# A Fourier mixing layer and a squared-ReLU FFN in one kernel: four steps of the third block and two more of the fourth in the halved form, the first folds and the even tables' weights in earlier steps

## The chip, the cores and the metric

The kernel runs on one core of a Trainium2 chip. The core has five engines, each with its own queue of instructions: PE (TensorE, the matrix engine), ACT (ScalarE), DVE (VectorE), POOL (GpSimd) and SP (SyncE), which here only issues stores. PE writes its sums to PSUM; ACT and DVE take them from there to SBUF, the on-chip memory. The metric is the device time of one launch in microseconds (us); lower is better.

## What is computed

The input x holds 8 batches of 3008 rows of 256 values. Each batch goes through a Fourier transform along the rows and one along the columns, of which only the real part is kept; the result goes row by row through two matrices (256 to 2048 and back) with a squared ReLU between them.

```python
X = np.fft.fft(x, axis=1)
X = np.fft.fft(X, axis=2)
x = X.real.reshape(B * S, D)          # 24064 x 256
h = np.maximum(x @ w_in, 0.0)         # 24064 x 2048
out = h * h @ w_out                   # 24064 x 256
```

## The kernel before

**Symmetry.** The real part of the transform of row k and that of row S - k are made of the same two sums, a cosine part P and a sine part Q: P + Q for one and P - Q for the other, up to the reversal of a row. So the kernel computes only 12040 columns (zc for the cosine part, zs for the sine part, of half of the columns each), and every column gives two output rows, an upper one and a mirrored one. The second transform is folded into the first matrix: `gh[:, 0]` and `gh[:, 1]` multiply zc and zs, and `gh[:, 2]` is `gh[:, 1]` with the factor that turns P + Q into P - Q (`turn2`). One output column needs a weight for a row of its own, `wv`, made by `row_weights` (L615).

**Blocks.** The 12040 columns go through 25 windows, here called blocks: `FIRST` gives 240, 512, 376, 376, 512, 448 columns (w = 0 to 5), then 512 each. The loop over `w` (L736) holds the whole order of work. A block has eight steps; step s makes 256 of the 2048 hidden values for all columns of the block. Between its matmuls stand those of other work, emitted by `others(s)` (L855): the jobs in `at[s]`, a slice of the second FFN matrix for the block before (`f2`, L667, sums po), the jobs in `post[s]`, and from step `lo` to `hi` a slice of the z jobs (L524, sums pz), which make zc and zs of a unit that the next block needs. Each engine takes its instructions in the order in which they are emitted.

**The plain step** (`pq`, `square`, `turn`): four matmuls (L787, L788) make P + Q in the sums ph, ACT takes them out with a ReLU (L797), two matmuls more (L793, the "turn") make P - Q of them in place, and ACT takes these out too. The squares of both are made by DVE (L802), but for the steps in `by_act`, where ACT squares the first half (L800). So a plain step has six matmuls as wide as the block, two evictions and two squares.

**The halved step** (`half_q`, `half_p`, `row_sum`, `halves`): two matmuls make Q alone, ACT takes it out as -2Q (`sn`, L820), two more add P, and ACT takes out P + Q (`hd`, L828). DVE makes P - Q by adding sn to hd (L850), takes the ReLU of both halves (L851) and squares them (L852). Ahead of that it adds the row of its own: `row` (L836) multiplies `eb` by a weight from `wv`, once for each 128 hidden values, and one add (L840) puts the rows on sn. Halved steps are grouped, in pairs at most, and DVE's three large operations are done once for a group, in the step after its last one. `eb` is the first row of zs spread over all partitions by a transfer that POOL issues (`row_spread`, L629), one for each block that has halved steps.

**Which steps.** `PLAN` (L60) maps a number to (groups of halved steps, steps with an ACT square), and `plan(w)` (L719) picks the number: none for w < 3, `PLAN[3]` for w = 3, that is (1, 2) and (4) halved and 0, 5, 6 squared by ACT, and `PLAN[2]` for w = 4, (2, 3) halved. In blocks 0 and 4, and in block 1, steps go in twos (`ng = 2`, L888).

**Folds and tables.** Each batch is loaded by POOL's queue into `xo` and folded by DVE along both axes (`fold_steps`, L376). The even half goes through DRAM and back (`even`, `back`, tile `rb`), and four last folds (`late`: two `fold8` L447, two `fold16` L458, and POOL's four small copies `nyq8` L464 to L466 into xt and spn) make what the z jobs of the even units read. The first batch's last folds stand in steps 3 to 6 of the third block (w = 2), the second's in steps 0 to 3 of the fifth (w = 4). `table_steps` (L244) makes the tables of sine and cosine for the even units, also in the third block: frequencies and arguments in step 0, turns (1), mods (2), absm (3), sine and cosine on ACT (4, 5), and the weights `weigh` (L285) in step 7. `row_weights` (16 matmuls, L619, and one DVE operation) stands in step 2.

**The z jobs.** `z_steps` (L504) makes one unit: for each part (0 cosine, 1 sine) and each half h a chain of matmuls. After h = 0 ACT copies the sums out (`es`, L529), after h = 1 it takes them out as zc or zs (L533), and DVE makes the mirrored columns from both (`minus`, L540). The order of parts and halves is one list for all units (L779): (1, 0), (0, 0), (1, 1), (0, 1). Of the even units, the sine part reads `spn` and the cosine part doesn't.

Of the kernel before, what the change touches and what calls it, by code (L numbers as in the profile page):

```python
# [28 lines left out]
def kernel(  # L29
# [30 lines left out]
    PLAN = {  # L60
# [5 lines left out]
    }  # L66

    RQ = (1, 3, 5, 0, 2, 4)
# [20 lines left out]
    def win_of(col):  # L89
        return max(w for w in range(NW) if wins[w][0] <= col) if col < TOT else NW  # L90
# [483 lines left out]
    f0s = fold_steps(0)  # L574
# [127 lines left out]
    folds = {0: f0s}  # L702

    def fold_jobs(i):
        f = folds[i] = fold_steps(i)
        return [f["d_even"], f["n_cos"], f["d_odd"], f["n_sin"], f["odds"], f["nyq"], f["even"], f["back"]]
# [11 lines left out]

    def plan(w):  # L719

        if w < 3:
            return (), ()
        if w < 5:
            return PLAN[3 if w == 3 else 2]
        first, late, main = w in first_at, w in late_at, w in fold_at
        n = 4 if main or late else 5 if first or w + 1 == NW or not need[w + 1] else 6
        return PLAN[n - (first and late)]

    def halved(w):

        return plan(w)[0]
# [4 lines left out]
    for w in range(NW):  # L736
# [4 lines left out]
        lo, hi = 0, NST - 2 if w == 3 or w > 4 else NST - 1  # L741
        at = [[] for _ in range(NST)]
        post = [[] for _ in range(NST)]
        if w == 0:
            at[7] = [f0s["even"], f0s["back"]]
        elif w == 1:
            fj = fold_jobs(1)
            at = [fj[0:1], fj[1:3], fj[3:4], fj[4:5], [], [], [], []]
            post[5] = fj[5:6]
            lo, hi = 6, 7  # L750
        elif w == 2:
            te = table_steps()
            at = [[folds[1]["even"], lambda: te["freq"](), lambda: te["args"](0)], [lambda: te["turns"](0)], [lambda: te["mods"](0)],
                  [lambda: te["absm"](0)], [lambda: te["sins"](0)], [lambda: te["coss"](0)], [], [lambda: te["weigh"]()]]
            for st in range(4):
                at[st + 3] = at[st + 3] + f0s["late"][st : st + 1]
            at[7].append(folds[1]["back"])
        elif w in fold_at:
            fj = jobs_of.pop(fold_at[w])
            at = [fj[2:3], fj[3:4], fj[4:5], [], [], [], fj[6:7], fj[7:8]]  # L760
            post[6] = fj[5:6]
        elif w == win_of(col_of[1, 1]) - 1:
            for st in range(4):
                at[st] = folds[1]["late"][st : st + 1]
            lo = 4
# [4 lines left out]
        if w in first_at:  # L770
            fj = jobs_of[first_at[w]] = fold_jobs(first_at[w])
            at[0] = at[0] + fj[0:1]
            at[1] = at[1] + fj[1:2]
        if w == 2:
            at[2].append(row_weights)
        zj, zl = [], []
        for u in need[w + 1]:
            zu = z_steps(u)
            zj += [(zu, 1, 0), (zu, 0, 0), (zu, 1, 1), (zu, 0, 1)]  # L779
        f2 = ffn2_steps(*old) if old else []  # L780
        phs = {}

# [20 lines left out]

        two = {s: g for g in halved(w) for s in g}
        by_act = plan(w)[1]
        sns, hds = {}, {}

# [178 lines left out]
```

## Time and profile before

| | before |
|---|---|
| median of 3 runs | 599.42 us (599.3 to 599.54) |
| the profiled execution | 599.14 us |
| its span | 597.4 us |
| busy PE, DVE, ACT, POOL | 97%, 86%, 86%, 17% of the span |
| granted TensorE clock | 0.999 |
| third block (w = 2), first L787 to the next block's | 48.27 to 70.28 us |
| fourth block (w = 3) | 70.28 to 89.93 us |
| fifth block (w = 4) | 89.93 to 112.55 us |

The profile is that of one execution. It times every instruction of each engine and says for idle time what ended it, by the semaphores. Lines such as L852 are those of the kernel below the heading above; a tile's name stands without its buffer number. Matmuls are pipelined: one that is listed with 0.32 us starts 0.16 us after the one ahead of it, and their ends are modelled, so that PE's busy time says only where it had work. The chain of waits follows the last instruction back to what released it, step by step, and so names what set the time at each moment. The time of a run is some 1.7 us more than the span of its instructions.

### The profile page before, as it was taken

The page shows a single profiled execution, that of the slowest core. Times are in us where ns is not written, and L with a number is a line of the kernel's source. Part 1 is how long each engine was busy: PE and PEld are TensorE (multiplying, and loading weights), DVE is VectorE, ACT ScalarE, POOL GpSimd, SP SyncE. Part 2 cuts the span into 40 slices and gives each one's busy share as a digit, 9 for nine tenths or more (in the row PEclk, how much of TensorE's full clock was granted, in tenths as well). Part 3 has the DMA queues.
Part 4 walks back from the last instruction along what each step waited for, and adds up shares of the span by engine and source line. Part 5 has one row for each costly group of instructions (what it writes and reads, how often), then busy time and mean ns, then how long its engine had stood idle before and what let it go on. Part 6 is the DMA issues. An engine that isn't in the chain of part 4 may idle for free.

```text
span 597.4 us, 11345 instructions
## 1 busy us (share of the span) xinstructions
PE 578.5 (97%) x4376; PEld 420.0 (70%) x4376; DVE 512.4 (86%) x748; ACT 514.3 (86%) x662; POOL 98.6 (17%) x152
## 2 busy tenths in 40 slices
PE   5899999999999999999999999999999999999996
PEld 2567776776777677777677777777777776776786
DVE  7897578886999987989889899898998799889980
ACT  7786888889999889989989898989989888888882
POOL 6350301202102023030112200403000120000000
PEclk9999999999999999999999999999999999999999
DMA  8955431562444536734455424555133351434122
GB/s 149 203 116 132 78 45 53 69 143 88 64 49 94 134 89 87 118 111 60 44 129 110 88 41 59 110 115 97 45 34 69 74 95 41 54 54 43 62 58 68
DMA packets 37581, 50.31 MB, mean 84 GB/s; under 512 B 4567, under 2 KB 30711, under 8 KB 37527
## 3 DMA queue, kind: packets, MB, share of 16 engines
q0 software_dynamic: 10400, 24.94, 32.1%
q1 hardware_dynamic: 26899, 24.44, 13.5%
q8 instruction: 34, 0.56, 0.4%
q10 hardware_dynamic: 228, 0.21, 0.1%
q14 instruction: 20, 0.16, 0.1%
HBM read 33.63 MB, written 27.84 MB: 103 GB/s over the span
## 4 chain that ended last, share of the span: by engine, by line
PE 66%; DVE 14%; ACT 11%; issue 7%; DMA 1%; POOL 0%; ACTq 0%; DVEq 0%; SPq 0%; POOLq 0%
PE po L667 39%; PE ph L826 5%; PE ph L812 5%; PE ph L793 4%; PE ph L787 4%; PE ph L788 4%; ACT h L797 3%; PE pz L524 3%; ACT sn L820 3%; DVE h L852 2%; ACT osb L682 2%; DVE hd L851 2%; ACT hd L828 2%; DVE hd L850 2%; DVE h L802 1%
## 5 line engine op out<-in xcount | busy, mean ns | idle before, releaser
L667 PE MATMUL po<-wout,h 128*128 128x256 f16 (+1 forms) x3024 | 362.0, 273 | 1.1 <-DVE h L852 1.1
L667 PEld LDWEIGHTS <-h 128*128 128x128 f16 (+1 forms) x3024 | 296.3, 98 | 73.0 <-DVE h L852 1.7
L797 ACT ACTIVATE h<-ph 128x1024 f16<-128x1024 f32 (+3 forms) x196 | 185.6, 981 | 11.6 <-PE ph L793 8.6
L828 ACT ACTIVATE hd<-ph 128x1024 f16<-128x1024 f32 (+3 forms) x94 | 94.0, 1001 | 14.7 <-PE ph L826 13.3
L852 DVE TENSOR_TENSOR h<-hd 128x4096 f16<-128x4096 f16 (+6 forms) x51 | 105.4, 2066 | 1.4
L802 DVE TENSOR_TENSOR h<-h 128x1024 f16<-128x1024 f16 (+3 forms) x135 | 85.4, 657 | 23.9 <-ACT h L797 22.4
L820 ACT ACTIVATE sn<-ph 128x1024 f16<-128x1024 f32 (+3 forms) x94 | 93.6, 997 | 0.7 <-PE ph L812 0.7
L840 DVE TENSOR_TENSOR sn<-sn,hd 128x2048 f16<-128x2048 f16 (+6 forms) x51 | 56.7, 1113 | 22.7 <-ACT sn L820 19.8
L682 ACT ACTIVATE osb<-po 128x512 f32<-128x512 f32 (+3 forms) x95 | 54.6, 578 | 24.6 <-PE po L667 23.9
L787 PE MATMUL ph<-zc,gh 128*128 128x512 f16 (+3 forms) x196 | 72.1, 368 | 0.5 <-ACT h L883 0.3
L788 PE MATMUL ph<-zs,gh 128*128 128x512 f16 (+3 forms) x196 | 72.1, 369 | 0.0
L850 DVE TENSOR_TENSOR hd<-hd,sn 128x2048 f16<-128x2048 f16 (+6 forms) x51 | 56.7, 1111 | 14.0 <-ACT hd L828 13.0
L800 ACT ACTIVATE h<-h 128x1024 f16<-128x1024 f16 (+3 forms) x61 | 62.7, 1028 | 1.9
L851 DVE TENSOR_SCALAR hd<-hd 128x4096 f16<-128x4096 f16 (+6 forms) x51 | 56.8, 1113 | 1.5
L826 PE MATMUL ph<-zc,gh 128*128 128x512 f16 (+3 forms) x188 | 54.6, 372 | 3.4 <-ACT sn L820 2.5
L793 PE MATMUL ph<-zs,gh 128*128 128x512 f16 (+3 forms) x196 | 55.3, 368 | 0.2 <-ACT h L797 0.2
L812 PE MATMUL ph<-zs,gh 128*128 128x512 f16 (+3 forms) x188 | 54.5, 373 | 0.0
L836 DVE TENSOR_SCALAR hd<-eb,wv 128x512 f16<-128x512 f16 (+3 forms) x188 | 54.0, 347 | 0.3 <-DMA eb<-zs 0.3
L788 PEld LDWEIGHTS <-gh 128*128 128x128 f16 x196 | 19.1, 97 | 21.2 <-issue 1.0
L787 PEld LDWEIGHTS <-gh 128*128 128x128 f16 x196 | 19.1, 97 | 20.3
L812 PEld LDWEIGHTS <-gh 128*128 128x128 f16 x188 | 18.3, 97 | 20.9
L629 POOL DMA_DIRECT2D eb<-zs x22 | 13.3, 603 | 117.4 <-ACT zs L533 59.4
(145 smaller groups left out, 418.0 us busy)
## 6 DMA issues: line engine op xcount, KB each, us to landing
out_dram<-osb SPq DMA_DIRECT2D x77, 128.0 KB
xo<-in_x_dram POOLq DMA_DIRECT2D x7, 768.0 KB, 7.3
scr<-ev POOLq DMA_DIRECT2D x8, 390.0 KB, 4.8
eb<-zs POOLq DMA_DIRECT2D x19, 128.0 KB, 7.0
rb<-scr POOLq DMA_DIRECT2D x16, 130.0 KB, 2.6
out_dram<-osb SPq DMA_DIRECT2D x12, 94.0 KB
w<-in_moe_w_in_dram POOLq DMA_DIRECT2D x2, 512.0 KB, 9.8
wout<-in_moe_w_out_dram POOLq DMA_DIRECT2D x1, 1024.0 KB, 11.8
```

Of the source, the lines that this page charges most:

```text
L667: nc.tensor.matmul(po[0:m, j * D : (j + 1) * D], h2[:, fc, q : q + m], wout16[:, fc, :], start=(fc == 0 and (j == 0 or not four or i > 3)) ...
L787: nc.tensor.matmul(ph[:, a, 0:wn], gh[:, 0, f0 : f0 + P], zcw[:, 0:wn], start=True, stop=False)
L788: nc.tensor.matmul(ph[:, a, 0:wn], gh[:, 1, f0 : f0 + P], zsw[:, 0:wn], start=False, stop=True)
L793: nc.tensor.matmul(phs[s][:, a, 0:wn], gh[:, 2, f0 : f0 + P], zsw[:, 0:wn], start=False, stop=True, skip_group_check=True)
L797: nc.scalar.activation(h1[:, :, 0:wn], phs[s][:, :, 0:wn], AF.Relu)
L802: return [lambda: nc.vector.tensor_tensor(h2[:, 2 * s : 2 * s + 2, sg * wn : (sg + 1) * wn], hv, hv, op=ALU.mult)]
L812: nc.tensor.matmul(ph[:, a, 0:wn], gh[:, 1, f0 : f0 + P], zsw[:, 0:wn], start=True, stop=True)
L820: nc.scalar.activation(sns[g][:, i : i + 2, 0:wn], ph[:, :, 0:wn], AF.Copy, bias=0.0, scale=-2.0)
L826: nc.tensor.matmul(ph[:, a, 0:wn], gh[:, 0, f0 : f0 + P], zcw[:, 0:wn], start=False, stop=True, skip_group_check=True)
L828: nc.scalar.activation(hds[g][:, i : i + 2, 0:wn], ph[:, :, 0:wn], AF.Copy, bias=0.0, scale=1.0)
L851: lambda: nc.vector.tensor_scalar(out=hv, in0=hv, scalar1=0.0, scalar2=None, op0=ALU.max),
L852: lambda: nc.vector.tensor_tensor(h2[:, 2 * g[0] : 2 * g[-1] + 2, 0 : 2 * wn], hv, hv, op=ALU.mult),
```

## The change

It changes the order of work in the third, fourth and fifth blocks and adds no instruction of a new kind.

- `plan(w)` gives w = 2 the new `PLAN[0]`: steps (2, 3) and (4, 5) halved, steps 0, 1, 6 and 7 with an ACT square. Before, all eight were plain, with all squares on DVE.
- w = 3 gets `PLAN[5]`: (1, 2), (3, 4) and (5) halved, ACT squares in 0, 6 and 7.
- Since the third block has halved steps, it also gets a row spread of its own, emitted in the second block, and the rows that come with it.
- In the third block the table steps, the first batch's last folds and `row_weights` are laid out anew: turns, `row_weights` and the first fold in step 1, mods and the second fold in 2, absm and sine in 3, cosine and the third fold in 4, weights and the last fold in 5, nothing in 6, the second batch's `back` in 7 as before.
- In the fifth block (the only one with `lo == 4`) the z jobs start with the cosine part's first half.

```diff
     PLAN = {
...
         2: (((2, 3),), ()),
+        0: (((2, 3), (4, 5)), (0, 1, 6, 7)),
     }
...
     def plan(w):
 
-        if w < 3:
+        if w < 2:
             return (), ()
         if w < 5:
-            return PLAN[3 if w == 3 else 2]
+            return PLAN[(0, 5, 2)[w - 2]]
...
         elif w == 2:
             te = table_steps()
-            at = [[folds[1]["even"], lambda: te["freq"](), lambda: te["args"](0)], [lambda: te["turns"](0)], [lambda: te["mods"](0)],
-                  [lambda: te["absm"](0)], [lambda: te["sins"](0)], [lambda: te["coss"](0)], [], [lambda: te["weigh"]()]]
-            for st in range(4):
-                at[st + 3] = at[st + 3] + f0s["late"][st : st + 1]
+            l8 = f0s["late"]
+            at = [[folds[1]["even"], lambda: te["freq"](), lambda: te["args"](0)], [lambda: te["turns"](0), row_weights, l8[0]],
+                  [lambda: te["mods"](0), l8[1]], [lambda: te["absm"](0), lambda: te["sins"](0)], [lambda: te["coss"](0), l8[2]],
+                  [lambda: te["weigh"](), l8[3]], [], []]
             at[7].append(folds[1]["back"])
...
-        if w == 2:
-            at[2].append(row_weights)
         zj, zl = [], []
         for u in need[w + 1]:
             zu = z_steps(u)
-            zj += [(zu, 1, 0), (zu, 0, 0), (zu, 1, 1), (zu, 0, 1)]
+            zj += [(zu, p, h) for p, h in (((0, 0), (1, 0), (1, 1), (0, 1)) if lo == 4 else ((1, 0), (0, 0), (1, 1), (0, 1)))]
```

## The prediction

> **What bounds the kernel now.** I read the page's head first, then the busy times by stretch for the blocks that the change touches, then the chain of waits and the timeline inside them.
>
> ```profile
> span 597.4 us, 11345 instructions
> ...
> PE 578.5 (97%) x4376; PEld 420.0 (70%) x4376; DVE 512.4 (86%) x748; ACT 514.3 (86%) x662; POOL 98.6 (17%) x152
> ```
>
> ```profile
> 48.27:70.28 22.01, 22.01 (x194) 17.61 (x192) 15.83 (x35) 15.56 (x24) 3.02 (x8) 1.00 0.38 83
> 70.28:89.93 19.65, 18.97 (x160) 15.01 (x158) 13.59 (x28) 16.90 (x27) 2.85 (x3) 1.00 0.42 63
> 89.93:112.55 22.62, 21.75 (x162) 15.13 (x160) 20.11 (x32) 19.28 (x27) 3.11 (x5) 1.00 0.25 51
> ...
> 135.00:300.00 165.00, 163.71 (x1228) 118.00 (x1227) 148.76 (x208) 150.49 (x186) 27.28 (x40) 1.00 0.48 86
> ```
>
> A stretch's row has its length, then the busy time of PE, weight loads, DVE, ACT and GpSimd, the granted clock and DMA. Each runs from a block's first matmul (L787) to the next one's: third block (w = 2), fourth, fifth, and a long steady stretch. In the third block TensorE (PE) is busy for 22.01 of 22.01 us and VectorE (DVE) and ScalarE (ACT) for some 16: there PE alone sets the time. In the fourth PE has 0.7 us of gaps, in the fifth 0.9, and DVE is at 20.1 of 22.6. The profiled execution took 599.14 us, 1.74 more than its span.
>
> ```profile
> 54.47 0.38 PE pv L619 x16
> ...
> 68.38 1.75 PE po L667 x16
> 70.13 0.32 PE ph L793 x2
> ```
>
> The chain of waits (start, duration, what) gives the price of PE work: sixteen FFN2 matmuls 1.75 us, two turns (L793, 376 columns) 0.32, the row weights (L619) 0.38.
>
> ```profile
> L797 ACT ACTIVATE h<-ph 128x752 f16<-128x752 f32 x15 | 11.2, 797 | 3.7 <-PE ph L793 3.7
> L802 DVE TENSOR_TENSOR h<-h 128x752 f16<-128x752 f16 x15 | 8.2, 550 | 5.9 <-ACT h L797 5.0
> ...
> L458 DVE TENSOR_TENSOR yt<-xt 128x520 f16<-128x520 f16 x2 | 0.8, 424 | 0.0
> ```
>
> The groups of the third block (busy time, mean ns of one, idle time before) show where its slack is: DVE idles 5.9 us ahead of its squares, waiting for ACT's evictions. That idle time is what the change can spend.
>
> **The turned matmuls that go.** A plain step issues six matmuls of 376 columns, a halved one four. Six steps become halved: 2 to 5 in the third block, 3 and 5 in the fourth. At 0.32 each the third block loses 4 x 0.32 = 1.3 us of PE work and the fourth 2 x 0.32 = 0.6. The 1.3 lies on the path, since PE has no gap there. Whether the 0.6 does depends on ACT and DVE, next.
>
> **ACT.** A halved step evicts twice, as a plain one does, at the same price (797 ns a relu above, 811 a half below). New are four squares (L800, 830 ns) in the third block, steps 0, 1, 6 and 7: 15.6 + 3.3 = 18.9 us of the 20.9 left. Going through the steps with these durations, each eviction that PE waits for (sn, before half_p) ends 0.1 to 0.4 us ahead of PE, also in steps 3 and 4, where sine and cosine stand between. I cost this at 0, bounds 0 and 0.6 (sn of steps 3 and 4 late by 0.3 each); the cover is the 1.75 us of FFN2 in each step, and a late eviction is paid in full. The fourth block keeps three ACT squares (step 7 for step 5).
>
> ```profile
> L800 ACT ACTIVATE h<-h 128x752 f16<-128x752 f16 x3 | 2.5, 830 | 0.1
> L828 ACT ACTIVATE hd<-ph 128x752 f16<-128x752 f32 x3 | 2.4, 811 | 0.2 <-PE ph L826 0.2
> ...
> L836 DVE TENSOR_SCALAR hd<-eb,wv 128x376 f16<-128x376 f16 x6 | 1.5, 313 | 0.3 <-DMA eb<-zs 0.3
> ...
> L840 DVE TENSOR_TENSOR sn<-sn,hd 128x1504 f16<-128x1504 f16 x1 | 0.9, 943 | 1.2 <-ACT sn L820 1.2
> L851 DVE TENSOR_SCALAR hd<-hd 128x3008 f16<-128x3008 f16 x1 | 0.9, 943 | 0.0
> ...
> L852 DVE TENSOR_TENSOR h<-hd 128x3008 f16<-128x3008 f16 x1 | 1.7, 1718 | 0.0
> ...
> L840 DVE TENSOR_TENSOR sn<-sn,hd 128x752 f16<-128x752 f16 x1 | 0.6, 551 | 0.1
> ...
> L285 DVE TENSOR_SCALAR sin<-sin,wge 128x377 f16<-128x377 f16 x2 | 0.6, 338 | 0.0
> ```
>
> **DVE.** Third block: twelve squares go (4 in the steps that ACT takes over, 8 in the halved ones): 12 x 0.55 = 6.6 us. Each pair brings four rows (1.0, from the timeline below), row sum 0.94, add of the halves 0.94, max 0.94, square 1.72: 5.5, twice 11.1. The weights of the even tables (0.6 us a table) move in from the block's end, where half of them ran past it: +0.6. Sum 15.8 - 6.6 + 11.1 + 0.6 = 20.9 us, as long as the whole block. So DVE uses up its idle time and ends the block behind. From the end of step 3's second eviction at 60.2 (by ACT's durations) it has pair (2, 3)'s 3.6, a fold 0.4, rows and sum 1.9, weights 1.2, a fold 0.4 and pair (4, 5)'s 3.6 ahead of it without a pause: 11.1, less 0.3 of overlap, so the square of pair (4, 5) is done at 71.0. PE first reads it in the fourth block's step 1, near 71.7: no wait, 0.7 us of cover. Fourth block: four squares go (2.2); the single (4,) becomes the pair (3, 4), 0.5 + 3 x 0.39 + 0.78 = 2.45 more, and the single (5,) adds 0.5 + 3 x 0.55 + half of 1.72 = 3.0; 0.6 of the weights leave. 13.6 + 2.6 = 16.2 of 18.8 us.
>
> ```profile
> 76.81 0.48 PE L826 MATMUL ph<-zc,gh 128*128 128x376 f16 x2 [0.19 <-ACT sn L820]
> ...
> 78.35 0.94 DVE L850 TENSOR_TENSOR hd<-hd,sn 128x1504 f16<-128x1504 f16 x1 [0.61 <-ACT hd L828]
> ...
> 81.77 0.48 PE L826 MATMUL ph<-zc,gh 128*128 128x376 f16 x2 [0.25 <-ACT sn L820]
> ...
> 86.40 0.61 DVE L540 SCALAR_TENSOR_TENSOR zc<-es,pz 128x135 f16<-128x135 f32 x2
> ...
> 86.92 0.48 PE L793 MATMUL ph<-zs,gh 128*128 128x376 f16 x2 [0.20 <-ACT h L797]
> ```
>
> What counts is when DVE writes the last part of zc (L540), for the fifth block's first matmul reads it. Before, that was 86.40 + 0.61 = 87.0, while PE came at 89.9: 2.9 us of cover. After: with PE 1.1 us ahead the add of pair (1, 2) starts at 78.35 - 1.1 = 77.2. Behind it on DVE stand 3.6 (pair's three), 1.0 and 0.94 (rows, sum of pair (3, 4)), 0.61 (zs), 3.6, 0.5 and 0.55 (pair (3, 4), single's rows and sum), 0.61 (zc): 11.4, less some 0.6 since back-to-back operations overlap (four rows of 313 ns take 1.00): zc at 88.0. PE, by its own work, is there at 88.0 too. So I keep the 0.6, with no cover left: from here a us later on DVE is a us on PE. PE's three stalls of the fourth block (0.19, 0.25 and 0.20 in the rows at 76.81, 81.77 and 86.92) stay, because they follow ACT in the steps with only eight FFN2 matmuls: 0.6 gained if all vanish, 0.6 lost if they double; I take 0.
>
> ```profile
> 53.55 0.60 ACT L682 ACTIVATE osb<-po 128x512 f32<-128x512 f32 x1 [0.90 <-PE po L667]
> ...
> 54.71 1.91 PE L667 MATMUL po<-wout,h 128*128 128x256 f16 x16
> ```
>
> **Row weights and folds.** L619 moves from step 2 to step 1 and still costs 0.38. In step 2 it covered the eviction of the FFN2 sums (53.55 + 0.60 = 54.15, before the FFN2 at 54.71), since the next FFN2 pair reuses that bank. Without it PE reaches that point 0.2 us before the eviction ends: +0.2 (bounds 0 and 0.6). The folds and the weights are DVE work counted above; the four small GpSimd copies behind the last fold come at the same time as before.
>
> ```profile
> 102.61 1.06 POOL L465 COPY spn<-yt 128x2 f16<-128x2 f16 x1 [2.54 <-DVE yt L458]
> ...
> 103.72 0.34 PE L524 MATMUL pz<-cos,spn 128*128 128x94 f16 x2 [0.33 <-POOL spn L465]
> ```
>
> **Order of z in the fifth block.** PE stood 0.33 us for the spn copy; with the cosine part first, four matmuls that read no spn go ahead of it and cover that: -0.3 (bounds 0 and -0.5).
>
> ```profile
> 46.25 0.48 ACT L533 ACTIVATE zs<-pz 128x376 f16<-128x376 f32 x1 [0.25 <-PE pz L524]
> ...
> 68.35 0.58 POOL L629 DMA_DIRECT2D eb<-zs  x1 [0.25 <-issue]
> ...
> 74.57 1.00 DVE L836 TENSOR_SCALAR hd<-eb,wv 128x376 f16<-128x376 f16 x4 [0.30 <-DMA eb<-zs]
> ...
> 84.37 0.55 DVE L850 TENSOR_TENSOR hd<-hd,sn 128x752 f16<-128x752 f16 x1
> 84.44 0.58 POOL L629 DMA_DIRECT2D eb<-zs  x1 [11.55 <-DVE zs L540]
> ...
> DMA to landing us min/median/max: 6.6/6.6/6.6
> ...
> DMA to landing us min/median/max: 5.9/6.9/10.6
> ```
>
> **Row spreads.** (The two lines on landing are the issue at 84.44 alone and all 22.) The third block now needs its own eb: one more GpSimd DMA at the end of the second block, issued near 46.9, when ACT has evicted zs (46.25 + 0.48). Even the longest landing, 10.6 us, gives 57.5, and its rows are due at 57.4: cost 0. The fourth block's eb is issued behind the last GpSimd copies, near 68.6 instead of 68.35; with 74.57 - 68.35 = 6.2 us, as now (DVE waits 0.30 for it), it lands at 74.8. Rows and sum take 1.9, so the add at 77.2 holds if it lands by 75.1. If a copy ahead of it takes 1.06 us, as the spn one at 102.61 did beside a DVE operation, that makes it some 75.6, 0.5 late. I take 0, bounds 0 and +0.9.
>
> **Into the sixth block.**
>
> ```profile
> 91.19 0.55 DVE L802 TENSOR_TENSOR h<-h 128x752 f16<-128x752 f16 x1 [1.51 <-ACT h L797]
> ...
> 93.39 0.69 DVE L802 TENSOR_TENSOR h<-h 128x1024 f16<-128x1024 f16 x1 [0.59 <-ACT h L797]
> ...
> 111.12 0.61 DVE L540 SCALAR_TENSOR_TENSOR zc<-es,pz 128x342 f16<-128x342 f32 x2
> ...
> 112.55 0.35 PE L787 MATMUL ph<-zc,gh 128*128 128x448 f16 x1
> ```
>
> From zc at 88.0 DVE has the single's 0.55, 0.55 and 0.86 and two squares of 0.5 left in the fourth block: 91.0. Two squares of 0.69 later, at 92.4, it begins the fifth block's folds, before at 93.39 + 0.69 = 94.1: 1.7 us sooner, because the 1.51 and 0.59 us of idle time go. PE's lead of 2.0 puts the sixth block at 110.5; zc is then ready at 111.7 - 1.7 = 110.0. The lead passes.
>
> **Sum.** -1.3 - 0.6 + 0.2 - 0.3 = -2.0 us: 599.14 - 2.0 = 597.1 for a profiled execution. The median of the runs stands 0.28 above the profiled one, so 597.4.
>
> **The rivals.** *DVE eats the fourth block's part.* DVE comes to zc 0.9 us late, by a slow copy ahead of eb or later evictions. For it: 16.2 busy us and no cover. Against: idle time ahead of the rows. Gain 2.0 - 0.9 = 1.1: 598.3.
>
> *The row spread turns slow, and the kernel slower.* The fourth block's eb lands at the longest landing, 68.6 + 10.6 = 79.2, which is 4.1 us past the last time that does no harm. All DVE work up to zc is 4.1 late; PE loses its 2.0 and 2.1 more: 599.4 + 2.1 = 601.5. It decides from a landing 2.0 past 75.1 on, at 77.1. For it: DVE, now without pauses from 67 to 72, runs beside this issue. Against: at 84.44 a spread was issued while DVE was busy without a pause from 84.37 to 87.0, and it landed in 6.6 us. A milder form: the spread starts when DVE pauses at 71.9 and lands at 78.1, 3.0 late: 600.4. The Trainium skill, "SBUF — State Buffer", section "SBUF: two separate sides", says that a DMA issued from GpSimd can't have its descriptors written while VectorE runs in a two-port mode, since one port pair is locked for the whole instruction. Taken strictly, with no gap between operations, that gives the milder form. The 6.6 us at 84.44 speak for short locks, not for one over a whole run of operations.
>
> *Given back later.* In the steady stretch PE idles 1.3 of 165 us and DVE is 90% busy; if some later wait has a time of its own, the lead goes: 599.4. Against: no order behind the fifth block changes, and every load is started by an instruction that comes earlier too.
>
> *More.* The gaps of both blocks (0.7 and 0.9, less the 0.33 counted) vanish too: 1.3 more, 596.1. For it: ACT starts the fourth block no later than before; against: its order there stays.
>
> **How the numbers follow.** Forecast 0.55, DVE's share 0.20, given back 0.08, the late spread 0.10 and its milder form 0.03, more 0.04. Under 0.2% (1.2 us) a measurement of this kernel can't tell a change from none, so faster means below 598.2. From the forecast 0.53 of 0.55 lie there, from DVE's share 0.09 of 0.20, and all of "more": 0.66. Slower (above 600.6) is the late spread alone, 0.10; the rest, the milder form among it, is 0.24. The range from 596.7 (stall and z bounds) to 599.5 holds the forecast, DVE's share and most of "given back".
>
> **What would show it.** L787 of the fourth block first at 69.2, of the fifth at 88.0, of the sixth at 110.5; PE still without a gap in the third block but for 0.2 us in step 2; DVE there at 20 us or more; the fourth block's rows (L836) by 75.1; zc (L540) at 88.0; no wait of PE for spn at the first z of the fifth block. If the fifth block starts after 88.9 with L540 just before it, DVE's rival holds; if L836 waits for eb beyond 77, the slower one. If DVE still shows several us of idle time in the third block while PE waits, the count of ACT was wrong.

## The result and the profile after

| | before | after |
|---|---|---|
| median | 599.42 us (7 runs, 599.30 to 599.54) | 597.47 us (7 runs, 597.20 to 599.15) |
| the profiled execution | 599.14 us | 597.29 us |
| its span | 597.4 us | 595.5 us |

The ratio of the times is 0.9971, 95% interval 0.9961 to 0.9981: 1.95 us less, where 2.0 were forecast. A second set of runs (`after_again`, timed beside two of the experiments) gave 597.35 against 599.37, 2.02 less. Now and then an execution of one of these kernels takes some 1.5 to 2 us longer at a granted clock of 0.995 to 0.997 (599.15 is one, at 0.996; the others of the changed kernel have 0.998 to 1.000), and the medians are not moved by them. In the changed kernel all lines below the new `PLAN` entry are shifted by one or so: L786 is the old L787, L541 the old L540, L849 to L851 the old L850 to L852, L835 the old L836, L525 the old L524, L630 the old L629, L668 the old L667. The kernels of the experiments have the changed kernel's numbers, but for z_alt_act07, z_alt_act06 and z_alt_osb_last, whose lines are shifted further.

Below stand the head of the profile's page and the busy times by stretch of the changed kernel: third, fourth and fifth block, again from a block's first L786 on (length, then busy time of PE, weight loads, DVE, ACT and POOL).

```profile
span 595.5 us, 11326 instructions
...
PE 577.0 (97%) x4364; PEld 419.2 (70%) x4364; DVE 519.7 (87%) x756; ACT 517.5 (87%) x666; POOL 98.1 (16%) x153
```

```profile
48.38:69.12 20.74, 20.74 (x186) 16.84 (x184) 18.36 (x38) 18.76 (x28) 2.59 (x6) 1.00 0.35 89
69.12:88.06 18.94, 18.34 (x157) 14.62 (x154) 15.94 (x29) 16.88 (x27) 4.00 (x6) 1.00 0.62 83
88.06:110.83 22.77, 21.62 (x162) 15.11 (x160) 22.40 (x37) 19.29 (x28) 3.12 (x5) 1.00 0.20 39
```

The third block is 22.01 - 20.74 = 1.27 us shorter and still without a gap of PE, the fourth 19.65 - 18.94 = 0.71 shorter, the fifth 0.15 longer. Over the whole kernel PE has twelve matmuls less (4364 for 4376). DVE has 2.5 us more in the third block, 2.4 more in the fourth, and now no pause of note in the fifth (22.40 of 22.77).

The same stretch in the timeline (start, duration, engine, line, tiles; in brackets the idle time ahead and what ended it):

```profile
68.29 0.94 DVE L850 TENSOR_SCALAR hd<-hd 128x3008 f16<-128x3008 f16 x1
...
68.36 0.99 POOL L630 DMA_DIRECT2D eb<-zs  x1
...
69.12 0.32 PE L786 MATMUL ph<-zc,gh 128*128 128x376 f16 x1
69.27 1.73 DVE L851 TENSOR_TENSOR h<-hd 128x3008 f16<-128x3008 f16 x1
...
71.66 0.60 PE L668 MATMUL po<-wout,h 128*128 128x256 f16 x4
...
75.00 1.00 DVE L835 TENSOR_SCALAR hd<-eb,wv 128x376 f16<-128x376 f16 x4 [1.90 <-DMA eb<-zs]
...
77.19 0.94 DVE L849 TENSOR_TENSOR hd<-hd,sn 128x1504 f16<-128x1504 f16 x1
...
87.53 0.61 DVE L541 SCALAR_TENSOR_TENSOR zc<-es,pz 128x135 f16<-128x135 f32 x2
...
88.06 0.38 PE L786 MATMUL ph<-zc,gh 128*128 128x512 f16 x1
...
89.37 0.38 PE L786 MATMUL ph<-zc,gh 128*128 128x512 f16 x1 [0.28 <-ACT h L796]
...
92.19 0.69 DVE L448 TENSOR_TENSOR xt<-rb 128x1040 f16<-128x1040 f16 x1
```

| event | forecast | measured |
|---|---|---|
| fourth block's first L786 | 69.2 | 69.12 |
| square of pair (4, 5) done | 71.0 | 69.27 + 1.73 = 71.00 |
| its first reader on PE | 71.7 | 71.66 |
| eb of the fourth block lands | by 75.1 (74.8) | 75.00 |
| add of pair (1, 2) | 77.2 | 77.19 |
| zc of the fifth block done | 88.0 | 87.53 + 0.61 = 88.1 |
| fifth block's first L786 | 88.0 | 88.06 |
| first fold of the fifth block | 92.4 | 92.19 |
| sixth block's first L786 | 110.5 | 110.83 |

The row for zc at 87.53 holds two operations (x2). The fifth block reads only what the first writes, 135 columns, and that one takes 0.29 us: its part of zc is ready at 87.82, 0.24 ahead of the block's first L786.

What the forecast missed stands in the fifth block, and in step 2 of the third. First the z jobs of the fifth block (timeline of the changed kernel):

```profile
100.80 1.06 POOL L466 COPY spn<-yt 128x2 f16<-128x2 f16 x1 [2.54 <-DVE yt L459]
...
105.04 0.24 PE L525 MATMUL pz<-sin,xt 128*128 128x188 f16 x1 [0.57 <-ACT es L530]
...
110.83 0.35 PE L786 MATMUL ph<-zc,gh 128*128 128x448 f16 x1
```

PE waits no longer for spn, but 0.57 us for es. The cause stands in the order of the list: both halves of one part go into the same sums pz, and ACT must have copied out the first half (es) before the second is added. With (0, 0), (1, 0), (1, 1), (0, 1) the two halves of the sine part are neighbours, so the copy has nothing to hide behind.

To follow the gain through, I compare the starts of the blocks, and behind them the starts of the same FFN2 matmul (there are 3024 in each kernel, in the same order). The changed kernel's execution is 0.11 us behind at the third block's start, 1.16 ahead at the fourth's, 1.87 at the fifth's, 1.72 at the sixth's, and from there stays between 1.71 and 1.80 ahead up to the last FFN2 matmul. So 1.27 + 0.71 - 0.15 = 1.83 of the 1.9 us come from the three blocks, and nothing is given back later.

### The profile page after: what moved, and what is told of

It reads as the page before. It is cut to its first block, busy times and chain, and to the rows that moved or that the text cites. A ratio compares the mean times of both kernels' runs of the same rounds, so it can differ in the third digit from the quotient of the medians.

```text
span 595.5 us, 11326 instructions
## 1 busy us (share of the span) xinstructions
PE 577.0 (97%) x4364; PEld 419.2 (70%) x4364; DVE 519.7 (87%) x756; ACT 517.5 (87%) x666; POOL 98.1 (16%) x153
## 4 chain that ended last, share of the span: by engine, by line
PE 69%; ACT 13%; DVE 10%; issue 5%; DMA 2%; SPq 0%; POOL 0%; ACTq 0%; DVEq 0%; POOLq 0%
PE po L668 41%; PE ph L825 6%; PE ph L811 5%; PE ph L786 4%; PE ph L787 4%; PE ph L792 4%; ACT h L796 4%; PE pz L525 3%; ACT sn L819 3%; ACT osb L683 2%; ACT hd L827 2%; DVE h L851 2%; DVE hd L850 1%; DVE hd L849 1%; DMA xo<-in_x_dram 1%
## 5 line engine op out<-in xcount | busy, mean ns | idle before, releaser
L668 PE MATMUL po<-wout,h 128*128 128x256 f16 (+1 forms) x3024 | 362.0, 273 | 1.1 <-DVE h L851 1.1
L668 PEld LDWEIGHTS <-h 128*128 128x128 f16 (+1 forms) x3024 | 296.4, 98 | 72.9 <-DVE h L851 1.7
L796 ACT ACTIVATE h<-ph 128x1024 f16<-128x1024 f32 (+3 forms) x184 | 176.7, 993 | 7.7 <-PE ph L792 3.9
L827 ACT ACTIVATE hd<-ph 128x1024 f16<-128x1024 f32 (+3 forms) x100 | 98.8, 989 | 16.4 <-PE ph L825 14.8
L851 DVE TENSOR_TENSOR h<-hd 128x4096 f16<-128x4096 f16 (+6 forms) x54 | 110.5, 2047 | 1.5
L819 ACT ACTIVATE sn<-ph 128x1024 f16<-128x1024 f32 (+3 forms) x100 | 98.5, 986 | 0.6 <-PE ph L811 0.6
L801 DVE TENSOR_TENSOR h<-h 128x1024 f16<-128x1024 f16 (+3 forms) x119 | 76.4, 670 | 14.3 <-ACT h L796 13.8
L839 DVE TENSOR_TENSOR sn<-sn,hd 128x2048 f16<-128x2048 f16 (+6 forms) x54 | 59.6, 1103 | 21.6 <-ACT sn L819 16.7
L849 DVE TENSOR_TENSOR hd<-hd,sn 128x2048 f16<-128x2048 f16 (+6 forms) x54 | 59.4, 1101 | 13.7 <-ACT hd L827 12.5
L786 PE MATMUL ph<-zc,gh 128*128 128x512 f16 (+3 forms) x184 | 68.2, 371 | 0.6 <-ACT h L882 0.3
L787 PE MATMUL ph<-zs,gh 128*128 128x512 f16 (+3 forms) x184 | 68.3, 371 | 0.0
L799 ACT ACTIVATE h<-h 128x1024 f16<-128x1024 f16 (+3 forms) x65 | 66.0, 1016 | 2.1
L850 DVE TENSOR_SCALAR hd<-hd 128x4096 f16<-128x4096 f16 (+6 forms) x54 | 59.6, 1104 | 1.6
L835 DVE TENSOR_SCALAR hd<-eb,wv 128x512 f16<-128x512 f16 (+3 forms) x200 | 57.0, 344 | 1.9 <-DMA eb<-zs 1.9
L811 PE MATMUL ph<-zs,gh 128*128 128x512 f16 (+3 forms) x200 | 57.4, 369 | 0.0
L792 PE MATMUL ph<-zs,gh 128*128 128x512 f16 (+3 forms) x184 | 52.3, 371 | 0.2
L630 POOL DMA_DIRECT2D eb<-zs x23 | 14.2, 619 | 123.2 <-ACT zs L534 66.5
L787 PEld LDWEIGHTS <-gh 128*128 128x128 f16 x184 | 18.0, 98 | 20.4 <-issue 1.0
L786 PEld LDWEIGHTS <-gh 128*128 128x128 f16 x184 | 17.9, 97 | 19.5
```

The source lines that it names most:

```text
L668: nc.tensor.matmul(po[0:m, j * D : (j + 1) * D], h2[:, fc, q : q + m], wout16[:, fc, :], start=(fc == 0 and (j == 0 or not four or i > 3)) ...
L786: nc.tensor.matmul(ph[:, a, 0:wn], gh[:, 0, f0 : f0 + P], zcw[:, 0:wn], start=True, stop=False)
L787: nc.tensor.matmul(ph[:, a, 0:wn], gh[:, 1, f0 : f0 + P], zsw[:, 0:wn], start=False, stop=True)
L792: nc.tensor.matmul(phs[s][:, a, 0:wn], gh[:, 2, f0 : f0 + P], zsw[:, 0:wn], start=False, stop=True, skip_group_check=True)
L796: nc.scalar.activation(h1[:, :, 0:wn], phs[s][:, :, 0:wn], AF.Relu)
L801: return [lambda: nc.vector.tensor_tensor(h2[:, 2 * s : 2 * s + 2, sg * wn : (sg + 1) * wn], hv, hv, op=ALU.mult)]
```

## The experiments

All are the changed kernel with one edit. Each was timed in five rounds beside the kernel before on the same chip; "against before" is the difference of the two medians there (the change itself: -1.95 and -2.02).

| kernel | median us | against before | ratio, 95% interval |
|---|---|---|---|
| third_plain | 598.68 | -0.63 | 0.9983 (0.9973 to 0.9992) |
| fourth_old | 598.10 | -1.21 | 0.9975 (0.9966 to 0.9984) |
| layout_old | 598.59 | -0.72 | 0.9984 (0.9975 to 0.9993) |
| z_old | 597.16 | -2.09 | 0.9964 (0.9951 to 0.9978) |
| z_alt | 596.59 | -2.66 | 0.9956 (0.9943 to 0.9970) |
| max_twice_third | 597.70 | -1.55 | 0.9974 (0.9963 to 0.9984) |
| max_twice_fourth | 597.76 | -1.49 | 0.9978 (0.9969 to 0.9987) |
| spread_late | 600.46 | +1.15 | 1.0022 (1.0011 to 1.0033) |
| z_alt_act07 | 596.65 | -2.72 | 0.9956 (0.9942 to 0.9969) |
| z_alt_act06 | 596.64 | -2.73 | 0.9954 (0.9941 to 0.9968) |
| z_alt_osb_last | 596.64 | -2.73 | 0.9948 (0.9935 to 0.9961) |
| after_again | 597.35 | -2.02 | 0.9966 (0.9952 to 0.9979) |

The intervals reach 0.6 to 0.8 us to each side, so a difference of a few tenths is read from the traces, by the starts of the same FFN2 matmuls. There two executions of the changed kernel (the first profile and after_again) differ by a constant 0.06 to 0.08 us, from the third block on to the end.

### Where the gain comes from: the two blocks one by one

```diff
 third_plain
-        if w < 2:
+        if w < 3:
             return (), ()
         if w < 5:
-            return PLAN[(0, 5, 2)[w - 2]]
+            return PLAN[(5, 2)[w - 3]]
 fourth_old
-            return PLAN[(0, 5, 2)[w - 2]]
+            return PLAN[(0, 3, 2)[w - 2]]
```

> The changed kernel with a plain third block (no halved steps, no ACT squares, no row spread of its own); the earlier folds, tables and weights stay, and so does the fourth block's new plan. The prediction's ledger: the four halved steps are worth 1.3 us: 598.8. Rival: the earlier folds and weights, not the matmuls, make the gain: 597.5 to 597.8.

> The changed kernel with the old plan of the fourth block: (1, 2) and (4) halved, ACT squares in 0, 5, 6. The prediction's ledger gives the fourth block's two steps 0.6 us: 598.1. Rival (DVE eats the fourth block's part): the two steps bring nothing, 597.5 or less.

Without the halved steps of the third block 2.02 - 0.63 = 1.4 us are gone (1.28 in the trace: 0.26 ahead of the change at that block's start, 1.02 behind at the next; the block is 22.01 us long, as before). Without the fourth block's new plan 2.02 - 1.21 = 0.8 are gone (0.72 in the trace). Both rivals fall: the matmuls that are no longer issued make the gain, and DVE doesn't eat the fourth block's part.

### What the earlier folds and weights are for

```diff
 layout_old
-            at = [..., [lambda: te["turns"](0), row_weights, l8[0]],
-                  [lambda: te["mods"](0), l8[1]], [lambda: te["absm"](0), lambda: te["sins"](0)], [lambda: te["coss"](0), l8[2]],
-                  [lambda: te["weigh"](), l8[3]], [], []]
+            at = [..., [lambda: te["turns"](0)],
+                  [lambda: te["mods"](0), row_weights], [lambda: te["absm"](0), lambda: te["sins"](0), l8[0]], [lambda: te["coss"](0), l8[1]],
+                  [l8[2]], [l8[3]], [lambda: te["weigh"]()]]
```

> The changed kernel with the first batch's last folds in steps 3 to 6, the weights of the even tables in step 7 and the row weights in step 2 of the third block, as they were; sine and cosine stay a step earlier, since the halved steps need the buffer of their arguments. Theory: the weights then stand on DVE behind the big square of pair (4, 5) and the last squares and end near 73.5, and PE's first z jobs of the fourth block (70.8) wait for them: 2.7 us later, 600.2. Rival: the places of folds and weights make no difference, 597.5.

The timeline of this kernel at the start of the fourth block:

```profile
71.56 0.54 DVE L286 TENSOR_SCALAR sin<-sin,wge 128x377 f16<-128x377 f16 x2
71.93 0.24 PE L525 MATMUL pz<-sin,xt 128*128 128x188 f16 x1 [1.14 <-DVE sin L286]
```

The wait is there and at the place named, PE for the weights, but it is 1.14 us and not 2.7, and the time is 1.3 us longer than that of the change (2.02 - 0.72). I had put the weights behind the last square and left out that without folds and weights ahead of it the large square itself comes 0.6 us sooner. So neither expectation (600.2 or 597.5) was met. The move of folds and weights gains nothing by itself, for third_plain has it too, and its third block is 22.01 us long as it was before; it keeps 1.1 to 1.3 us that the halved steps would give back.

### The order of the z jobs

```diff
 z_old
-... (((0, 0), (1, 0), (1, 1), (0, 1)) if lo == 4 else ((1, 0), (0, 0), (1, 1), (0, 1)))
+... ((1, 0), (0, 0), (1, 1), (0, 1))
 z_alt
-... (((0, 0), (1, 0), (1, 1), (0, 1)) if lo == 4 else ...
+... (((0, 0), (1, 0), (0, 1), (1, 1)) if lo == 4 else ...
```

> The changed kernel with the old order of the z jobs in the fifth block (sine part's first half first). The prediction's step: the new order is worth 0.3 us, so this one stands at 597.8. Theory from the trace of the changed kernel: the new order puts the two halves of the sine part next to each other, PE then waits 0.57 us for es (105.04 us, released by ACT L530), more than the 0.33 us that the wait for spn took before, so the old order is 0.1 to 0.3 better: 597.2 to 597.4, with a wait of PE for spn of some 0.3 us in the profile and none for es.

> The changed kernel with a third order of the z jobs in the fifth block: cosine first half, sine first half, cosine second half, sine second half. Theory: neither the wait for spn nor the one for es is left, PE gets the 0.57 us back: 596.9, with the sixth block's first L786 near 110.3. Rival: the next wait takes its place (zc from DVE, or ACT's evictions), no gain: 597.4 to 597.5.

The timeline with the old order, and below it with the third one:

```profile
101.82 0.34 PE L525 MATMUL pz<-cos,spn 128*128 128x94 f16 x2 [0.39 <-POOL spn L466]
...
110.65 0.35 PE L786 MATMUL ph<-zc,gh 128*128 128x448 f16 x1
```

```profile
108.80 0.60 DVE L541 SCALAR_TENSOR_TENSOR zc<-es,pz 128x342 f16<-128x342 f32 x2
109.32 0.60 DVE L541 SCALAR_TENSOR_TENSOR zs<-es,pz 128x342 f16<-128x342 f32 x2
...
110.10 0.35 PE L786 MATMUL ph<-zc,gh 128*128 128x448 f16 x1
```

With the old order PE waits 0.39 us for spn and none for es, and the sixth block starts at 110.65, 0.18 sooner than in the change. This execution was 0.09 us ahead already at the third block's start, so the old order is 0.09 better, not 0.3 worse. With the third order both waits are gone: 110.83 - 110.10 = 0.73 us sooner, and 0.7 of it is there at the end (span 594.8). zs is ready at 109.92, 0.2 us ahead of that L786 and 0.4 ahead of its own reader behind it, so only a few tenths more are to be had here before DVE holds PE. This version beats both kernels.

### How much cover DVE has

The same operation, the max of a pair, is done a second time: once in the third block, once in the fourth. It changes no value.

```diff
-                lambda: nc.vector.tensor_scalar(out=hv, in0=hv, scalar1=0.0, scalar2=None, op0=ALU.max),
+                lambda: [nc.vector.tensor_scalar(out=hv, ..., op0=ALU.max) for _ in range(2 if w == 2 and g == (2, 3) else 1)],
```

(In max_twice_fourth the condition is `w == 3 and g == (3, 4)`.)

> The same operation once more (0.94 us), but in the third block, for the pair (2, 3). The prediction's ledger has 0.7 us of cover ahead of PE's first read of the square of pair (4, 5), and idle time of DVE (1.9 us) ahead of the rows of the fourth block, so only 0 to 0.3 us should go onto the time: 597.5 to 597.8. Rival: DVE, busy without a pause from 61 to 72 us, is the bound there, and the whole 0.9 is paid: 598.4.

> The changed kernel with one more DVE operation: the max (L850) of the fourth block's pair (3, 4) is done twice, 0.94 us, the output stays the same. Prediction's step: DVE has no cover left ahead of zc in the fourth block, so 0.7 to 0.9 us go onto the time: 598.2 to 598.4, with the fifth block starting at 88.8 or later behind L541. Rival: ACT sets the end of the fourth block (the chain of waits names ACT from 83 to 89 us) and DVE still has cover: under 0.2, 597.5 to 597.7.

The timeline of max_twice_third, then that of max_twice_fourth:

```profile
70.13 1.73 DVE L851 TENSOR_TENSOR h<-hd 128x3008 f16<-128x3008 f16 x1
...
71.92 1.27 PE L668 MATMUL po<-wout,h 128*128 128x256 f16 x10 [0.20 <-DVE h L851]
```

```profile
88.45 0.61 DVE L541 SCALAR_TENSOR_TENSOR zc<-es,pz 128x135 f16<-128x135 f32 x2
...
88.79 0.39 PE L786 MATMUL ph<-zc,gh 128*128 128x512 f16 x1 [0.63 <-DVE zc L541]
...
89.67 0.38 PE L786 MATMUL ph<-zc,gh 128*128 128x512 f16 x1
```

Two max operations take 1.92 us on DVE where one takes 0.94, so 0.98 is added. In the third block it costs 0.37 in the trace: the square ends at 71.86 and PE's first reader, without it at 71.66, starts at 71.92 (this execution began 0.11 sooner than the change's, so it is 0.37 late and not 0.26). The cover of 0.66 us (71.66 - 71.00) was right; the cost is a little over the stated 0.3 and far from the whole. In the fourth block it costs 0.45 and not 0.7 to 0.9, and 597.76 is close to the rival's 597.5 to 597.7. zc does set PE's first L786 (88.79 for 88.06), but the second group starts only 0.30 later (89.67 for 89.37), because in the change PE stands there anyway for ACT's last relu of the block. So some 0.5 of the 0.98 us are covered: 0.2 ahead of the first L786, since only the first part of zc counts, and the rest in that wait for ACT. The ledger saw neither, and the second sits behind the point that I looked at.

### The slower rival, forced

```diff
 spread_late (the spread is no longer issued at step hi - 1 of w = 2)
-            at[7].append(folds[1]["back"])
+            at[7] += [folds[1]["back"], lambda: row_spread(3)]
```

> The changed kernel with the fourth block's row spread (eb) issued behind the second batch's four transfers from DRAM, so near 73.2 us instead of 68.4: it lands some 4.8 us later, near 79.6. The slower rival's price: a spread that lands 4.5 us past 75.1 makes all DVE work up to zc that late, and PE with it, as there is no cover: 597.5 + 4.4 = 601.9. Rival: half of it is taken up by slack of DVE further on: 599.7.

Its timeline:

```profile
73.11 0.60 POOL L630 DMA_DIRECT2D eb<-zs  x1
...
78.59 1.00 DVE L835 TENSOR_SCALAR hd<-eb,wv 128x376 f16<-128x376 f16 x4 [5.52 <-DMA eb<-zs]
...
91.06 0.61 DVE L541 SCALAR_TENSOR_TENSOR zc<-es,pz 128x135 f16<-128x135 f32 x2
...
91.41 0.39 PE L786 MATMUL ph<-zc,gh 128*128 128x512 f16 x1 [2.16 <-DVE zc L541]
```

The spread lands 3.6 us later (78.6 for 75.0), zc is 3.5 us later (91.06 for 87.53), and the time is 3.1 to 3.2 longer than that of the change (3.0 in the trace): kernel before + 1.15. That lies between the two expectations, 601.9 and 599.7. So the mechanism of the slower rival is real, and its price is one for one past the same half a us of cover. It didn't happen in the change because the spread landed 6.6 us after its issue.

### What holds the end of the fourth block

The chain of waits of the change runs over ACT from 83 to 89 us. Two kernels take one ACT square of the fourth block away from ACT, a third changes ACT's order at the end of the block; all three have the third order of the z jobs. (The diff is shortened, the last one to its sense.)

```diff
 z_alt_act07, z_alt_act06 (PLAN[1] used for w = 3 alone)
+        1: (((1, 2), (3, 4), (5,)), (0, 7)),     # act06: (0, 6)
 z_alt_osb_last
-                osb = ...; eviction; stores          # as the last FFN2 job is emitted
+                behind.append(out)                   # run after square(7, 1)
```

> The third order of the z jobs, and ACT squares of the fourth block only in steps 0 and 7; the first square of step 6 goes to DVE. Theory: ACT sets the end of the fourth block from 83 to 89 us (the chain of waits), without the 0.83 of that square PE starts the fifth block's second L786 group up to 0.45 sooner, and the square, 0.45 on DVE, stands behind zc, where DVE has time: 596.1 to 596.3 against 596.6 for the third order alone. Rival: DVE is the bound (it had no pause from 77 to 92), the square delays the fifth block's folds and zc: 596.6 to 597.1.

> The same with ACT squares of the fourth block in steps 0 and 6, and step 7's first square on DVE. The same two theories: 596.1 to 596.3, or 596.6 to 597.1; with ACT as the bound, both kernels should gain alike, as both squares stand ahead of the last eviction of the fourth block.

> The third order of the z jobs, and the last eviction of FFN2 sums in the fourth block (osb, two ACT operations, 0.64 us) stands behind the last relu of the block in place of ahead of it. Theory: taking an ACT square away brought nothing, so not ACT's load but the order at the end of the block holds PE: FFN2 ends, then the two osb, then the last relu, and only then PE's second L786 group of the fifth block. With the relu first that group starts at 89.0 in place of 89.4, and the time is 0.3 lower: 596.3. Rival: PE's next wait (for sn, 96.3 us) or zc takes the gain back: 596.6.

The chain of waits of z_alt_act07 at the block's end ("issue" is time in which the engine waited for nothing that the profile shows), then ACT's timeline in z_alt_osb_last:

```profile
86.12 1.76 PE po L669 x16
87.88 0.02 issue
87.90 0.66 ACT osb L684 x2
88.56 0.69 ACT h L797
89.25 0.04 issue
89.30 0.38 PE ph L787
```

```profile
88.37 0.80 ACT L803 ACTIVATE h<-ph 128x752 f16<-128x752 f32 x1 [0.17 <-PE ph L799]
89.06 0.65 ACT L686 ACTIVATE osb<-po 128x256 f32<-128x256 f32 x2
89.59 3.99 ACT L803 ACTIVATE h<-ph 128x1024 f16<-128x1024 f32 x4
```

None of the three gains: 596.64 and 596.65 beside the 596.6 of z_alt. Without the square the chain is no longer ACT's, but PE's FFN2 runs up to 87.9, and behind it come osb and the last relu all the same: the wait follows from the order, not from ACT's load. So my theory of ACT's load fell. DVE, the rival, isn't the bound either: with the square on it in z_alt_act07 zc of the sixth block starts 0.34 us later (109.14 for 108.80), and the sixth block begins at 110.06, no later than the 110.10 of z_alt. With osb behind the relu PE's second group does start 0.26 us sooner (89.22 for 89.37, in an execution that began 0.11 later), but then ACT's four relus of 1024 columns run without a pause from 89.59 on, and most of the gain is gone at PE's turn matmuls by 91.6. As far as these runs show, the stall at the start of the fifth block is a round trip between PE and ACT that these edits only move; what would remove it stays open.

### The change once more

> The changed kernel itself once more, beside the runs of the other two on the same chip: 1.9 to 2.0 us under the kernel before. All theories agree.

It gave 597.35 against 599.37: 2.02 less, as far as the intervals tell the same as the first 1.95.

## Why the prediction was right

- **The matmuls that go.** 1.3 us in the third block: 1.27 in the trace, 1.28 by undoing it. 0.6 in the fourth: 0.71, and 0.72 by undoing it. These are the two large terms, and they were worked out from the rows of PE's own work. Of the fourth block's 0.71, 0.63 are PE's busy time; the rest are its gaps, which I had left as they were and which went from 0.68 to 0.60.
- **ACT.** Cost 0 in the third block: right, PE has no gap there.
- **DVE's ledger.** The times of the four events that I had named (71.0, 77.2, 88.0, 92.4) came within 0.2 us. The sum for the third block, 20.9 us, was too large as a busy time of that block: 18.4, so my sign of "20 us or more" did not come. Part of the work that I counted runs after it, the square of pair (4, 5) from 69.27 on among it.
- **"From here a us later on DVE is a us on PE."** This step failed: some 0.5 us are free, as both max_twice_fourth and spread_late show. I had dated the last part of zc, and the fifth block's first matmul reads the part before it; and I had not looked at PE's next wait, for ACT. It changed nothing in the total, because in the change DVE's zc came in time.
- **The row weights, +0.2.** This step failed. I had said that without them PE meets the eviction of the FFN2 sums, "since the next FFN2 pair reuses that bank". In the changed kernel that eviction and the next FFN2 stand so:

```profile
54.07 0.60 ACT L683 ACTIVATE osb<-po 128x512 f32<-128x512 f32 x1 [0.44 <-PE po L668]
...
54.50 1.69 PE L668 MATMUL po<-wout,h 128*128 128x256 f16 x14
```

  The matmuls start at 54.50 (x14, because the view ends at 56 us), the eviction ends at 54.67: they don't wait for it, so the premise of the same bank doesn't hold. Measured: 0. layout_old, with the row weights back in step 2, has a third block of the same 20.74 us. The semaphores in the traces agree: the first of these matmuls waits for one of DVE, the engine that reads the row weights' sums pv (L621, done at 53.21), while in the kernel before it waits for one of ACT. That fits a bank taken over from pv, whose reader now stands ahead of the eviction in the order of emission; which bank it is, no view names.
- **The order of z, -0.3.** This step failed too, in its sign. The wait for spn did go, but I looked only at the job that had waited and not at the ones that the new order makes neighbours. Measured: 0.1 lost by z_old. The fifth block is 0.15 longer than before; the 0.06 beyond that I did not trace.
- **The sum.** -1.3 - 0.6 + 0.2 - 0.3 = -2.0 was forecast; -1.27 - 0.71 + 0 + 0.1 = -1.9 was found. The two wrong steps were +0.2 and -0.3 in the sum and nearly cancel there, so the total is right by 0.1 with small terms that aren't: for these, that was luck.
- **The rivals.** "DVE eats the fourth block's part": no, by fourth_old. "Given back later": no, by the count through the kernel. "The row spread turns slow": it landed at 75.0, 0.1 ahead of the limit of 75.1, and spread_late shows the price where it doesn't. Its milder form didn't come about: DVE ran from 67.3 to 71.9 without a pause, and the spread still landed 6.6 us after its issue. I had got that form from the Trainium skill's "SBUF — State Buffer" ("SBUF: two separate sides") by letting the lock hold over a whole run of operations. "More": PE's gaps didn't vanish; they are 0.60 us in the fourth block and 1.15 in the fifth, before 0.68 and 0.87.

## What to carry to other kernels

Price a change of this kind by the work that the bounding engine no longer issues, and then date the few events where another engine hands over to it; a ledger of busy times by block says which engine, but only such dates say whether there is cover. Cover can also sit behind the point that is looked at: the next wait of the same engine, for a third one, makes the first part of a delay free. When the order of jobs is changed to remove a wait, list which jobs become neighbours, above all two that use the same accumulator; here the order that kept both pairs apart was worth 0.7 us more than the one chosen.

## What the hardware showed that I had not expected

In these runs a transfer issued from GpSimd while DVE runs a long tensor-scalar operation is held for that operation and no longer. The issue of eb (L630) at 68.36 took 0.99 us in place of 0.60, and ended at 69.35, 0.12 after DVE's max (L850, 68.29 to 69.23). At the next DVE operation (the square L851, two inputs, 69.27 on) the GpSimd queue went on at once. The same 0.99 beside the same max stands in fourth_old (68.38) and max_twice_third (69.23). At 0.4 us it is far smaller than a wait for DVE's pause at 71.9. This agrees with the lock "for the whole instruction" of the Trainium skill, "SBUF — State Buffer" ("SBUF: two separate sides"), if the max runs in one of the modes that are meant there, which no view here says.

Beside a DVE operation with two inputs the transfer is not held, but a small copy on GpSimd is, as the timeline of the changed kernel shows:

```profile
67.32 0.93 DVE L849 TENSOR_TENSOR hd<-hd,sn 128x1504 f16<-128x1504 f16 x1
67.54 0.77 POOL L466 COPY spn<-yt 128x2 f16<-128x2 f16 x1 [9.44 <-DVE yt L459]
68.24 0.19 POOL L467 COPY spn<-yt 128x2 f16<-128x2 f16 x1
...
83.27 0.93 DVE L849 TENSOR_TENSOR hd<-hd,sn 128x1504 f16<-128x1504 f16 x1
83.34 0.57 POOL L630 DMA_DIRECT2D eb<-zs  x1 [10.18 <-DVE zs L541]
```

Beside the add of the halves the issue at 83.34 took 0.57 us. The copy at 67.54 took 0.77 and ended 0.06 after the add, where the like copy behind it took 0.19. Of the 32 copies of this kind (L465 to L467) in this trace, 29 end within 0.1 us behind a DVE operation during which they ran. The copy of spn in the fifth block is such a one, 1.06 us long (100.80), and it would be worth moving it away from that add; no run does so, so it is not shown that PE's wait for spn would go.
